# Reordering the first batch of a fused attention and phase-mixing kernel

## The chip, the cores and the metric

The kernel runs on one core of one Trainium2 chip, in one launch. The metric is the device time of that launch in microseconds. Times before are 173.44, 174.29 and 175.55 us; the median is 174.29 us.

## The reference

There are two stages. The first is attention over `q`, `k`, `v` of shape (4 batches, 8 heads, 768 positions, 64 channels), in which a query sees only the first 8 keys (the global ones) and the 96 keys up to its own position. Each head subtracts a slope times the distance from the scores.

```python
scores = scale * (q @ k.T) - slope[h] * dist      # dist = n_local for global keys out of the band
scores = where(is_global | is_local, scores, -1e9)
x = softmax(scores) @ v                           # heads side by side: (4, 768, 512)

theta = x @ w_theta
y = w_tok_r @ (x * cos(theta)) + w_tok_i @ (x * sin(theta))   # over the 768 positions
u = x + y
out = u + maximum(u @ w_ch, 0)
```

## The kernel before, in words

**Tiles.** Positions are dealt to 128 partitions, six to each, so a head pair's q or k is a tile of 128 rows by 2 x 384 columns. TensorE transposes it into `qT` and `kT` (channels of the two heads on the partitions). `GROUPS` splits the band of scores of a head pair into three groups of 128x128 blocks: group 0 (three blocks), groups 1 and 2 (four blocks each). A block is either the diagonal one or the one before it. For the blocks before the diagonal of query tiles 2 to 5, `kT` has four extra tiles of 128 columns (`kT[:, S:]`): a copy of key tiles 1 to 4 with the first 8 columns overwritten by the global keys (`att_extras`, lines 231 to 238, the "key copies"). `prepare_v` (lines 88 to 94) makes the same kind of copy of v, `v_pv`.

**Weights of the scores.** Distances come into the scores in one of two ways. In batch 0, groups 0 and 2 get a bias on TensorE (`att_bias`, line 252, with the scaled identities `ident_d`), then ScalarE makes the exponential `p` (line 275). Everywhere else ScalarE makes the exponential `e` (line 279) and VectorE multiplies it by `wmask` (`att_mul`, lines 290 and 292).

**Stages of a head pair.** `att_transpose` (transposes on line 215, copies out of PSUM on line 225, kT by ScalarE, qT by VectorE), key copies, `att_scores` for three groups, `att_values` (line 319), `att_norm` (lines 335, 337) and `turn_x` (line 351), which turns the result for the product with `w_theta` (`mix_theta`, line 368). ScalarE makes cosine and sine (lines 376, 377), VectorE `mix_z` (line 384). `setup_wtok` turns the two position weights into `w_tokT` (TensorE line 114, copy line 117 by VectorE or line 119 by ScalarE). `mix_tok` (line 403) and `mix_ch` (line 445) are the large products.

**Order.** Each operation goes through `K`, which keeps the written order on its engine: the lists at lines 506 to 576 (batch 0) and 578 to 604 are the schedule. `attend_beside` weaves the next batch's attention into the products of this one. Tiles named with `bufs=2` have two places; a third allocation waits until the first is read for the last time. Those that matter here are `ps_w` (wide score and theta tiles), `ps_tr` (transposes), `ps_mm`, and `kT`.

**Loads.** The first head pair of q and k comes as f32 over the SP and ScalarE queues (line 142) and is cast by VectorE (line 509). All other loads are issued by GpSimd (lines 75, 80, 102) on one queue, in the order of lines 153 to 158, then `load_wtok(0)`, `load_wtok(1)`, batch 1, `w_ch`. GpSimd also makes most key copies, between those issues. `keep_warm` (line 137) issues matmuls on zeros.

Of the kernel before, what the change touches and what calls it, by code (L numbers as in the profile page):

```python
# [16 lines left out]
def kernel(  # L17
# [13 lines left out]
    nc = tc.nc  # L31
# [72 lines left out]
    def load_wtok(wi):  # L104
        w_nats[wi] = mbuf.tile([T, NT, S], BF, name="w_nat", tag="zri", bufs=3)
        load_weight(w_nats[wi], (moe_w_tok_r, moe_w_tok_i)[wi])
# [34 lines left out]
    for src, dst, queue in ((q, first[:, 0], nc.sync), (k, first[:, 1], nc.scalar)):  # L141
        K(queue.dma_start(out=dst, in_=src[0, 0:2].rearrange("h (p t) d -> p h (t d)", t=NT)))
# [7 lines left out]
    keep_warm(8)  # L150
# [80 lines left out]
    def att_extras(b, h0, eng=nc.gpsimd, values=True):  # L231
        kT = kTs[b, h0]
        K(eng.tensor_copy(out=kT[:, S:], in_=kT[:, T:S - T]))  # L233
        K(eng.tensor_copy(
            out=kT[:, S:].rearrange("a (t p) -> a t p", p=T)[:, :, 0:NG],
            in_=kT[:, None, 0:NG].to_broadcast([T, NT - 2, NG])))
        if eng is nc.gpsimd and values:
            prepare_v(b, h0)
# [16 lines left out]
    def att_scores(b, h0, g_, mul=True):  # L255
# [3 lines left out]
        bias = b == 0 and g_ != 1  # L259
# [246 lines left out]
    for h in range(H):  # L506
        make_wmask(h)
# [3 lines left out]
    att_transpose(0, 0, extras=False, between=lambda: keep_warm(1), cuts=(43, T))  # L511
    make_ident_d(2, 6)
    att_extras(0, 0, nc.vector)
    prepare_v(0, 0, nc.vector)
    keep_warm(1)
    att_scores(0, 0, 0)
    att_scores(0, 0, 1)
    att_transpose(0, 2, extras=False)
# [4 lines left out]
    for h0 in (2, 4, 6):  # L523
        att_scores(0, h0, 0)
        att_scores(0, h0, 1, mul=False)
        att_values(0, h0 - 2, apart=True)
        att_norm(0, h0 - 2)
        att_norm(0, h0 - 1)
        if h0 < 6:
            att_transpose(0, h0 + 2)  # L530
            if h0 == 2:
                load_wtok(1)
            else:
                load_heads(1, 0, 4)
        att_mul(0, h0, 1)
        att_scores(0, h0, 2)
        if h0 < 6:
            turn_x(0, h0 // 2 - 1, False)
# [3 lines left out]
    turn_x(0, 2, False, nc.scalar.copy)  # L542
# [26 lines left out]
    setup_wtok(1, 3, "dve", False)  # L569
# [3 lines left out]
    mix_tok(0, 0, [(4, 0), (5, 0), (2, 1), (3, 1)])  # L573
    mix_tok(0, 1, [(4, 0), (5, 0), (2, 1), (3, 1)])
    setup_wtok(1, 4, "dve", False)
    setup_wtok(1, 5, "dve", False)
# [63 lines left out]
```

## Time and profile before

| what | value |
|---|---|
| median of three runs | 174.29 us |
| the profiled execution's own time | 173.54 us |
| its span, first to last instruction | 171.8 us |
| TensorE busy (matmul) | 162.1 us, 94% |
| VectorE / ScalarE / GpSimd busy | 114.2 / 103.0 / 60.9 us |
| granted TensorE clock | 1.000 over the span |

Times are microseconds from the first instruction; "idle before" is time in which an engine had nothing to do, with the instruction that ended it. PE is the matmul side of TensorE, PEld its weight loads, DVE VectorE, ACT ScalarE, POOL GpSimd, SP the engine of the other DMA queue. [...] 1.7 us of the profiled time (173.54 less 171.8) lie around the span.

### The profile page before, as it was taken

The numbers are of one execution on the slowest core, as the hardware profiler recorded it, in microseconds if no ns is written. First come the engines' busy times: TensorE is split into PE (matmuls) and PEld (weight loads), VectorE is DVE, ScalarE is ACT, GpSimd is POOL, SyncE is SP. The second block draws the span as 40 slices with busy tenths as digits, with TensorE's granted clock in tenths as the row PEclk, the third lists the DMA queues.
The fourth block names the chain that finished last, engine by engine and source line by source line (L and its number), as shares of the span: only waits on it lengthen the run. The fifth ranks groups of instructions, "written<-read, shape, count | busy, mean of one in ns | idle before, by whom it ended". The sixth has DMA issues, their size and how long they took to land.

```text
span 171.8 us, 4076 instructions
## 1 busy us (share of the span) xinstructions
PE 162.1 (94%) x1700; PEld 87.5 (51%) x1700; DVE 114.2 (67%) x210; ACT 103.0 (60%) x120; POOL 60.9 (35%) x99
## 2 busy tenths in 40 slices
PE   7669999999999999999999998999999999999992
PEld 2246665556465654536556553545655544444441
DVE  7878865965858774767587694748567766634362
ACT  5969887947676562798658604798756708400010
POOL 8996797004672820033944700044134000000000
PEclk9999999999999999999999999999999999999999
DMA  5999999999999999910699999911433642233325
GB/s 151 188 170 189 209 211 209 196 183 179 173 142 148 114 229 199 250 64 4 81 167 118 152 210 197 213 65 22 89 77 94 84 152 86 96 34 61 103 109 185
DMA packets 57058, 24.05 MB, mean 140 GB/s; under 512 B 43088, under 2 KB 54096, under 8 KB 57040
## 3 DMA queue, kind: packets, MB, share of 16 engines
q0 software_dynamic: 35328, 12.45, 69.2%
q1 hardware_dynamic: 21440, 10.95, 29.6%
q10 hardware_dynamic: 272, 0.39, 0.7%
q8 instruction: 13, 0.21, 0.6%
q14 instruction: 5, 0.04, 0.1%
HBM read 25.69 MB, written 6.29 MB: 186 GB/s over the span
## 4 chain that ended last, share of the span: by engine, by line
PE 76%; DMA 9%; DVE 6%; POOL 3%; ACT 2%; issue 2%; DVEq 0%; POOLq 0%; ACTq 0%
PE ps_mm L403 34%; PE ps_mm L445 11%; PE ps_w L368 10%; PE ps_w L270 6%; PE ps_tr L215 6%; DMA uTd<-u 5%; PE ps_w L319 4%; DMA v_sb<-in_v_dram 4%; DVE w_tokT L117 2%; PE ps_mm L319 2%; PE ps_tr L114 1%; DVE zri L384 1%; ACT e L279 1%; DVE p L292 1%; ACT kT L225 1%
## 5 line engine op out<-in xcount | busy, mean ns | idle before, releaser
L403 PE MATMUL ps_mm<-zri,w_tokT 128*128 128x512 bf16 x288 | 68.7, 380 | 0.1
L279 ACT ACTIVATE e<-ps_w 128x1024 bf16<-128x1024 f32 (+1 forms) x40 | 37.1, 958 | 18.4 <-PE ps_w L270 18.4
L403 PEld LDWEIGHTS <-w_tokT 128*128 128x128 bf16 x288 | 26.2, 98 | 30.7 <-issue 2.3
L233 POOL COPY kT<-kT 128x512 bf16<-128x512 bf16 x15 | 9.6, 643 | 68.8 <-ACT kT L225 68.7
L292 DVE TENSOR_TENSOR p<-e,wmask 128x1024 bf16<-128x1024 bf16 x28 | 19.9, 709 | 12.2 <-ACT e L279 12.2
L376 ACT ACTIVATE cs<-ps_w,halfpi 128x1024 bf16<-128x1024 f32 x12 | 13.4, 1116 | 19.9 <-PE ps_w L368 19.8
L408 DVE TENSOR_TENSOR u<-x_sb,ps_mm 128x512 bf16<-128x512 bf16 x24 | 16.2, 683 | 12.5 <-PE ps_mm L403 12.5
L368 PE MATMUL ps_w<-w_theta_bf,xT 128*128 128x512 bf16 x96 | 22.8, 379 | 0.3 <-ACT cs L377 0.3
L445 PE MATMUL ps_mm<-w_ch_bf,uTd 128*128 128x512 bf16 x88 | 22.5, 379 | 0.5 <-DMA uTd<-u 0.5
L384 DVE TENSOR_TENSOR zri<-cs,x_sb 128x1024 bf16<-128x1024 bf16 x24 | 16.1, 690 | 9.7 <-ACT cs L376 8.4
L270 PE MATMUL ps_w<-qT,kT 64*128 64x128 bf16 (+1 forms) x320 | 16.0, 223 | 2.8 <-DVE qT L225 1.3
L448 DVE SCALAR_TENSOR_TENSOR o_sb<-ps_mm,u 128x512 f32<-128x512 f32 (+2 forms) x25 | 16.5, 665 | 1.1 <-PE ps_mm L445 0.9
L270 PEld LDWEIGHTS <-kT 64*128 64x128 bf16 x320 | 9.3, 94 | 12.8 <-issue 8.5
L225 ACT COPY kT<-ps_tr 128x768 bf16<-128x768 bf16 (+2 forms) x17 | 12.9, 765 | 2.9 <-PE ps_tr L215 2.8
L319 PEld LDWEIGHTS <-p 128*128 128x128 bf16 x352 | 12.7, 97 | 3.7 <-DVE p L292 0.5
L368 PEld LDWEIGHTS <-xT 128*128 128x128 bf16 x96 | 8.9, 98 | 10.9 <-issue 0.5
L445 PEld LDWEIGHTS <-uTd 128*128 128x128 bf16 x88 | 8.1, 97 | 9.9 <-DMA uTd<-u 1.2
L80 POOL DMA_DIRECT2D v_sb<-in_v_dram x10 | 13.1, 1309 | 0.0
L377 ACT ACTIVATE cs<-ps_w 128x1024 bf16<-128x1024 f32 x12 | 12.2, 1020 | 0.0
L327 DVE TENSOR_TENSOR x_sb<-ps_w,rec 128x768 bf16<-128x768 f32 x12 | 11.5, 958 | 0.4
L319 PE MATMUL ps_w<-v_sb,p 128*128 128x65 bf16 x168 | 10.3, 193 | 0.0
L430 ACT COPY uT<-ps_tr 128x512 bf16<-128x512 bf16 x1 | 0.6, 586 | 15.5 <-PE ps_tr L426 15.5
(79 smaller groups left out, 189.5 us busy)
## 6 DMA issues: line engine op xcount, KB each, us to landing
out_dram<-o_sb SPq DMA_DIRECT2D x23, 256.0 KB, 3.0
q_sb<-in_q_dram POOLq DMA_DIRECT2D x6, 384.0 KB, 7.7
k_sb<-in_k_dram POOLq DMA_DIRECT2D x6, 384.0 KB, 10.4
v_sb<-in_v_dram POOLq DMA_DIRECT2D x6, 384.0 KB, 15.1
w_nat<-in_moe_w_tok_r_dram POOLq DMA_DIRECT2D x1, 1152.0 KB, 12.5
w_nat<-in_moe_w_tok_i_dram POOLq DMA_DIRECT2D x1, 1152.0 KB, 13.6
v_sb<-in_v_dram POOLq DMA_DIRECT2D x4, 192.0 KB, 7.2
q_sb<-in_q_dram POOLq DMA_DIRECT2D x3, 192.0 KB, 6.7
```

The costliest lines, as they stand in the source:

```text
L225: K(op(out=dst.rearrange("a (p t) -> a p t", t=NT)[:, p0:p1, :], in_=src.rearrange("a (t p) -> a p t", t=NT)[:, p0:p1, :]))
L270: K(nc.tensor.matmul(ps[:, hh, i_ * T:(i_ + w) * T], lhsT=kT[R, kc:kc + T], rhs=qT[R, it * T:(it + w) * T], start=not bias, stop=not bias ...
L279: K(nc.scalar.activation(e[:, :, 0:n * T], ps[:, :, 0:n * T], AF.Exp, scale=scale))
L292: K(nc.vector.tensor_mul(p.rearrange("a h (r x) -> a h r x", r=2), e.rearrange("a h (r x) -> a h r x", r=2), wmask[:, hs, None, T:3 * T].t ...
L319: K(nc.tensor.matmul(dst, lhsT=lhsT, rhs=rhs, start=(i_ == 0), stop=(i_ == len(mms) - 1)))
L368: K(nc.tensor.matmul(pth[:, s2, :], lhsT=xTs[b][:, dc, c:c + T], rhs=w_theta_bf[:, dc, :], start=(dc == 0), stop=(dc == NC - 1)))
L376: K(nc.scalar.activation(cs[:, :, 0, :], pth, AF.Sin, bias=halfpi))
L384: K(nc.vector.tensor_mul(zris[b][:, st:st + 2, wi, :].rearrange("a s (c d) -> a s c d", d=T), cs[:, :, wi, :].rearrange("a s (c d) -> a s ...
L403: K(nc.tensor.matmul(acc, lhsT=w_tokT[wi][:, st, tt * T:(tt + 1) * T], rhs=zris[b][:, st, wi, :], start=(done[b, tt] == 0), stop=(done[b, ...
L408: K(nc.vector.tensor_add(us[b][:, tt, :].rearrange("a (c d) -> a c d", d=T), x_sb[b][:, :, tt, :], acc.rearrange("a (c d) -> a c d", d=T)))
L445: K(nc.tensor.matmul(pc[:, 0:N], lhsT=uT[:, c:c + T], rhs=w_ch_bf[:, dc, cols], start=(dc == 0), stop=(dc == NC - 1)))
L448: K(nc.vector.scalar_tensor_tensor(o_sb, in0=pc[:, 0:N], scalar=0.0, in1=us[b][:, tt, cols], op0=ALU.max, op1=ALU.add))
```

## The change

All of it but the last hunk is in batch 0's attention.

- The first loads of q and k are split by head: head 0 on the SP queue, head 1 on the ScalarE queue, q ahead of k on both. Seven warm matmuls are issued instead of eight.
- `att_transpose(0, 0)` cuts its copies at column 64 of 128 instead of 43, and its key copies are made in two parts of two tiles each.
- Only six of eight `wmask` are made ahead; the last two stand behind the first scores and behind the transposes of pair 4.
- Pair 0's v copies on VectorE stand behind the transposes of pair 2; the scaled identities are made in two portions at other places.
- While pairs 2 and 4 are at their scores, the transposes of the next pair stand ahead of `att_values` of the pair before, not behind it. In pair 0 the multiplication of group 1 moves behind the transposes of pair 2.
- Pair 6's group 0 has no bias: it is multiplied by `wmask` on VectorE.
- `turn_x(0, 0)` and `(0, 1)` stand later, and `turn_x(0, 2)` is copied by VectorE instead of ScalarE.
- Two of the `w_tokT` copies go from VectorE to ScalarE, and the last two are set up four matmuls earlier.

```diff
+    for src, dst in ((q, first[:, 0]), (k, first[:, 1])):
+        for hh, queue in enumerate((nc.sync, nc.scalar)):
+            K(queue.dma_start(out=dst[:, hh, :], in_=src[0, hh].rearrange("(p t) d -> p (t d)", t=NT)))
...
-    keep_warm(8)
+    keep_warm(7)
...
+    def att_extras(b, h0, eng=nc.gpsimd, values=True, parts=1):
+        n = (NT - 2) // parts
+        for t0 in range(0, NT - 2, n):
+            dst = kT[:, S + t0 * T:S + (t0 + n) * T]
+            K(eng.tensor_copy(out=dst, in_=kT[:, (t0 + 1) * T:(t0 + 1 + n) * T]))
+            K(eng.tensor_copy(out=dst.rearrange("a (t p) -> a t p", p=T)[:, :, 0:NG],
+                in_=kT[:, None, 0:NG].to_broadcast([T, n, NG])))
...
-        bias = b == 0 and g_ != 1
+        bias = b == 0 and (g_ == 2 or g_ == 0 and h0 < H - 2)
...
-    for h in range(H):
+    for h in range(6):
         make_wmask(h)
...
-    att_transpose(0, 0, extras=False, between=lambda: keep_warm(1), cuts=(43, T))
-    make_ident_d(2, 6)
-    att_extras(0, 0, nc.vector)
-    prepare_v(0, 0, nc.vector)
-    keep_warm(1)
-    att_scores(0, 0, 0)
-    att_scores(0, 0, 1)
-    att_transpose(0, 2, extras=False)
+    att_transpose(0, 0, extras=False, between=lambda: keep_warm(1), cuts=(64, T))
+    keep_warm(1)
+    att_extras(0, 0, nc.vector, parts=2)
+    make_ident_d(2, 2)
+    att_scores(0, 0, 0)
+    make_wmask(6)
+    att_scores(0, 0, 1, mul=False)
+    att_transpose(0, 2, extras=False)
+    att_mul(0, 0, 1)
+    prepare_v(0, 0, nc.vector)
+    make_ident_d(4, 4)
     att_extras(0, 2, nc.gpsimd, False)
     prepare_v(0, 2)
     load_wtok(0)
     att_scores(0, 0, 2)
+    for h0 in (2, 4):
         att_scores(0, h0, 0)
         att_scores(0, h0, 1, mul=False)
+        att_transpose(0, h0 + 2)
+        if h0 == 2:
+            make_wmask(7)
+            load_wtok(1)
+        else:
+            load_heads(1, 0, 4)
         att_values(0, h0 - 2, apart=True)
+        att_mul(0, h0, 1)
         att_norm(0, h0 - 2)
         att_norm(0, h0 - 1)
         att_scores(0, h0, 2)
+        if h0 == 4:
+            turn_x(0, 0, False)
+    att_scores(0, 6, 0)
+    att_scores(0, 6, 1, mul=False)
+    turn_x(0, 1, False)
+    att_values(0, 4, apart=True)
+    att_norm(0, 4)
+    att_norm(0, 5)
+    att_mul(0, 6, 1)
+    att_scores(0, 6, 2)
...
-    turn_x(0, 2, False, nc.scalar.copy)
+    turn_x(0, 2, False)
...
-    setup_wtok(1, 3, "dve", False)
+    setup_wtok(1, 3, "act", False)
...
     mix_tok(0, 0, [(4, 0), (5, 0), (2, 1), (3, 1)])
+    setup_wtok(1, 4, "dve", False)
+    setup_wtok(1, 5, "act", False)
     mix_tok(0, 1, [(4, 0), (5, 0), (2, 1), (3, 1)])
-    setup_wtok(1, 4, "dve", False)
-    setup_wtok(1, 5, "dve", False)
```

More of the change, by code (lines that the diff above doesn't have):

```diff
@@ L140 @@
     first = mbuf.tile([T, 2, 2, NT * D], FP, name="first", tag="zri", bufs=3)
-    for src, dst, queue in ((q, first[:, 0], nc.sync), (k, first[:, 1], nc.scalar)):
-        K(queue.dma_start(out=dst, in_=src[0, 0:2].rearrange("h (p t) d -> p h (t d)", t=NT)))
+    for src, dst in ((q, first[:, 0]), (k, first[:, 1])):
+        for hh, queue in enumerate((nc.sync, nc.scalar)):
+            K(queue.dma_start(out=dst[:, hh, :],
+                              in_=src[0, hh].rearrange("(p t) d -> p (t d)", t=NT)))
     K(nc.scalar.activation(halfpi_e, halfpi, AF.Exp))
@@ L229, in att_transpose @@
             att_extras(b, h0)
-    def att_extras(b, h0, eng=nc.gpsimd, values=True):
+    def att_extras(b, h0, eng=nc.gpsimd, values=True, parts=1):
         kT = kTs[b, h0]
[L233 to L236, printed above, removed]
+        n = (NT - 2) // parts
+        for t0 in range(0, NT - 2, n):
+            dst = kT[:, S + t0 * T:S + (t0 + n) * T]
+            K(eng.tensor_copy(out=dst, in_=kT[:, (t0 + 1) * T:(t0 + 1 + n) * T]))
+            K(eng.tensor_copy(
+                out=dst.rearrange("a (t p) -> a t p", p=T)[:, :, 0:NG],
+                in_=kT[:, None, 0:NG].to_broadcast([T, n, NG])))
         if eng is nc.gpsimd and values:
@@ L522 @@
     att_scores(0, 0, 2)
-    for h0 in (2, 4, 6):
+    for h0 in (2, 4):
         att_scores(0, h0, 0)
         att_scores(0, h0, 1, mul=False)
+        att_transpose(0, h0 + 2)
[4 more added lines that the diff above has]
+            load_heads(1, 0, 4)
         att_values(0, h0 - 2, apart=True)
+        att_mul(0, h0, 1)
         att_norm(0, h0 - 2)
         att_norm(0, h0 - 1)
[L529 to L535, printed above, removed]
-        att_scores(0, h0, 2)
-        if h0 < 6:
-            turn_x(0, h0 // 2 - 1, False)
+        att_scores(0, h0, 2)
+        if h0 == 4:
[8 more added lines that the diff above has]
+    att_scores(0, 6, 2)
     load_heads(1, 4, 4)
```

## The prediction

> **What bounds the kernel now.** I read the windows first. From 40 to 168 us TensorE is busy 127.02 of 128 us (127.42 of the sum row less 0.40 of the last window) at full clock, with the same large products behind the change as before it. So what the change is worth is the shift of TensorE's work at about 45 us, and nothing that happens ahead of it counts unless it is still there then.
>
> ```profile
> sum 132.00, PE 127.42 PEld 66.92 DVE 84.71 ACT 72.08 POOL 34.06; mean PE 3.86 PEld 2.03 DVE 2.57 ACT 2.18 POOL 1.03
> 168.00:172.00 4.00, 0.40 (x5) 0.21 (x3) 0.76 (x2) 0.00 (x0) 0.00 (x0) 0.97 0.48 174
> ```
>
> Then the chain that ended last, at its start. The reader is to see that v of pair 0 lands at 9.53 and that VectorE's queue, in order, puts the v copies and a multiplication ahead of pair 2's qT, for which TensorE waits until 12.52 us.
>
> ```profile
> 3.03 6.50 DMA v_sb<-in_v_dram
> ...
> 9.55 0.72 DVE v_pv L91
> ...
> 10.29 0.71 DVE v_pv L92
> 11.01 0.59 DVE p L292
> 11.60 0.88 DVE qT L225
> ...
> 12.52 0.56 PE ps_w L270 x12
> ```
>
> Third the timeline of GpSimd (start, length). Its DMA issues follow one another from 1.48 to 10.89 us; only then comes pair 2's key copy, though kT has been ready since 10.92 at the latest.
>
> ```profile
> 9.05 1.08 POOL L80 DMA_DIRECT2D v_sb<-in_v_dram  x1
> 10.07 0.82 POOL L102 DMA_DIRECT2D w_theta_bf<-in_moe_w_theta_dram  x1
> 10.99 1.08 POOL L233 COPY kT<-kT 128x512 bf16<-128x512 bf16 x1
> 12.13 0.21 POOL L234 COPY kT<-kT 128x32 bf16<-128x32 bf16 x1
> ```
>
> Last ScalarE's timeline at the seam to batch 1: it is idle 2.3 us, copies kT, loads the table for Exp, and the first exponential waits for TensorE, not for the table.
>
> ```profile
> 37.78 0.80 ACT L225 COPY kT<-ps_tr 128x768 bf16<-128x768 bf16 x1 [2.30 <-PE ps_tr L215]
> 38.60 1.28 ACT L279 ACT_TABLE_LOAD   x1
> 40.50 0.81 ACT L279 ACTIVATE e<-ps_w 128x768 bf16<-128x768 f32 x1 [0.62 <-PE ps_w L270]
> 41.73 1.94 ACT L279 ACTIVATE e<-ps_w 128x1024 bf16<-128x1024 f32 x2 [0.42 <-PE ps_w L270]
> ```
>
> **The start, to 12.3 us.** The four first loads carry the same bytes; q's halves now lead on both queues. q landed 4.3 us after its issue at 0.74, k 4.6; with q first it lands between 3.9 (half of the bytes) and 5.05 (no gain), and k stays at 5.34. VectorE is busy with the identities until 4.28 anyway. The second issue on ScalarE's queue costs 0.48 us, ahead of a first `wmask` that waits for `dist` until 3.61 while the table load and dummy end at 2.74: hidden with 0.4 us to spare. k's cast ends at 5.95 instead of 6.33, k's transposes at about 6.55. ScalarE, which before made eight masks until 7.02, makes six (0.426 us each) until 6.2 and is free then. kT's parts of 384 columns: between the 0.38 us of 258 columns and the roughly 0.5 of 510, so 7.05 and 7.46. Key copies in parts let group 1 begin at 7.6 instead of 8.77. But mask 6 (0.43) now stands ahead of its exponential: that starts at 8.6 instead of 9.21, and kT of pair 2 is ready at 10.3 instead of 10.92. VectorE no longer waits for v here: qT of pair 2 is ready at 9.35 instead of 12.47, and group 0 of pair 2 runs at 10.4 instead of 12.52.
>
> There the next wait takes over. Group 1 of pair 2 needs GpSimd's key copies, which cannot begin before 10.89: by the rows they end at 12.34, or 11.85 if the large copy takes 0.61 as later copies do (VectorE's two-input multiplication is no longer beside it). Before, this group ran at about 12.8. So up to 3.1 us gained on VectorE become 0.4 to 0.9 on TensorE, and it hardly matters how early q lands.
>
> **12.3 to 27.5 us.** I follow the order with the rows' paces: exponential 0.92 (four blocks) or 0.71 (three), kT 0.74, qT 0.86, multiplication 0.65, the four norm operations 1.42, turned copy 0.48 on VectorE; TensorE 0.79 for 24 transposes, 0.76 for a bias and eight scores, 0.75 for values, 0.34 for a turn.
> Group 1 of pair 2 ends 12.75; pair 4's q and k have landed (11.93 and 12.92), transposes to 13.55, exponential 12.8 to 13.8, kT 14.5 (before 15.54). Mask 7 (0.43) fits into ScalarE's wait for group 2, whose scores end at 15.05 behind the values. Group 0 of pair 4 15.4 to 15.75; group 1 waits for a `ps_w` place (group 2's exponential, 16.12), runs at 16.17 against 16.88. Transposes of pair 6 16.5 to 17.3 (k landed 16.14), kT 18.45 (before 19.77). Group 0 of pair 6 at 19.15, without its two bias matmuls (0.32 us saved), group 1 at 19.9 (before 21.11), exponentials of pair 6 to 21.5 (before 22.74).
> Now VectorE binds: behind the exponential of group 0 at 20.57 it has the added multiplication (0.55), a turned copy (0.48), norms 1.42, multiplication 0.65, then the turned copy taken over from ScalarE (0.5): 24.2. Norms of pair 6 begin at 24.15 instead of 24.73, the last turn at 25.75 instead of 26.3, theta ends 27.5 instead of 28.2. Of 1.2 us at 21 us, **0.6 us** is left: two VectorE operations, 1.05 us, stand on the path there; their cover, VectorE's two waits of 0.53 before values, is used up.
>
> **27.5 to 40 us** has the same chain of sines, `zri` and weight copies, so the shift stays. The landings leave room: `w_tok_r` 26.03 for 27.4, `w_tok_i` 31.6 for 32.8, batch 1's k 35.5 for 36.6. The copy of weight tile 3 on ScalarE falls into its 2.3 us of idleness and costs nothing.
>
> **The seam.** Weight tiles 4 and 5, set up four matmuls earlier, take away TensorE's two short waits there (0.04 and 0.08 us idle in the windows of half a microsecond from 40 to 41). But tile 5's copy by ScalarE (0.75) now stands between kT and the table load. With the shift of 0.6 it runs 38.7 to 39.45, the load to 40.74, first exponential to 41.56. Group 2 needs that tile's `ps_w` place, so it starts at 41.6, no earlier than before; the two next exponentials end at 43.4 against 43.68, the multiplication behind them at 44.1, and values at 44.15 instead of 44.45. **0.6 becomes 0.27**; with the faster GpSimd copy 0.8 becomes 0.47. I take 0.3.
>
> The loads at 1.25 and 25.21 us last 1.28 and the next activation follows 0.01 us behind, so I add no pause behind the load. [...]
>
> **Sum.** The profiled execution took 173.54 us: 171.8 of span and 1.7 around it. Less 0.3 that is 173.2. Its time lies 0.75 under the median; against 174.29 I forecast **174.0 us**.
>
> **Rivals.**
> 1. *The earlier gain survives the seam.* If ScalarE's copy of tile 5 runs without delaying the table (kT copied earlier), the shift at values is the full 0.6 to 0.8 and the two waits at 40 us (0.1) go: 0.7 to 0.9 us, or, if VectorE's added 1.05 is hidden too, up to 1.4; no more, since batch 1's k at 35.5 stops it. 172.9 to 173.6, taken as 173.4. For it: the idle 2.3 us on ScalarE. Against: the load stands last in the order. Chance 0.2.
> 2. *Slower: VectorE between 20.6 and 24.2 us.* The same instructions took 0.93 and 0.96 us (multiplications at 15.83 and 20.02) while GpSimd copied, against 0.67. If the three operations there run at such a pace, 0.3 each, the shift at 28 us falls from 0.6 to -0.3, and the seam's 0.33 comes on top: 0.6 us slower, 174.9. It decides from the point where less than 0.33 of shift is left at 37 us. For it: GpSimd's v copies for pair 6 run until 21. Against: they end before most of that strip. Chance 0.25.
> 3. *The change moves nothing*: GpSimd's issues last longer, group 1 of pair 2 stays at 12.8, and the seam is no later because the copy fits: 174.3. Chance 0.1.
> 4. *A pause behind the Exp load.* That load ended at 39.88 and its exponential began at 40.50, so a pause of up to 0.62 isn't excluded there; it would now be on the path: 0.3 gained less 0.62 is 0.3 us slower, 174.6. The two other loads speak against it; chance 0.02.
>
> The forecast itself has 0.43. 1% here, 1.7 us, is about what a measurement of this kernel can tell from no change: the three runs lie 2.1 us apart. All cases are inside it; what lies beyond is the scatter of the median and an unknown cost at either side. Faster by over 1%: 0.06; within: 0.85; slower: 0.09. The range holds rivals 1 to 3 and half a microsecond of scatter on either side: 172.7 to 175.2.
>
> **What would show it.** Pair 2's first scores near 10.4, its group 1 at 11.9 to 12.4 behind GpSimd's small copy; TensorE idle 1.2 to 1.7 us between them; theta's last product of the first four columns near 27.5; the Exp table load near 39.5 with an exponential right behind it; values of batch 1 near 44.1. I am wrong if the table load isn't what the first exponential waits for, if the first 45 us are shifted by over a microsecond, or if TensorE has new waits behind them.

## The result, and the profile after

The changed kernel takes 174.14 us (median of 22 runs, 173.68 to 175.46), the kernel before, run beside it, 173.33 us (22 runs, 172.83 to 175.55). The ratio is 1.0043, with an interval of 1.0024 to 1.0061: the change makes the kernel **0.75 us slower** (0.42 to 1.06), where 0.3 us faster was forecast. That the forecast of 174.0 us lies near 174.14 is luck: the median of the three runs of before that it was set against lay 1 us above the median of 22. The profiled execution of after took 174.62 us, with a span of 172.7.

The windows of after, in the same form as those shown of before (window, its length, then busy time and instructions of PE, PEld, DVE, ACT, POOL, granted clock, DMA share, GB/s):

```profile
40.00:168.00 128.00, 124.06 (x1216) 65.97 (x1235) 82.43 (x133) 72.74 (x81) 33.51 (x57) 1.00 0.88 122
168.00:172.00 4.00, 0.93 (x8) 0.47 (x6) 1.25 (x3) 0.00 (x0) 0.00 (x0) 1.00 0.54 200
```

TensorE is 3 us less busy than before in the same 128 us, but the trace also holds 30 matmul records fewer (1216 for 1246), so this difference can't be read as waiting. What is new is read from the waits of TensorE instead, here from 20 to 70 us of after (engine, tile and line, what was waited for: us in total, times, longest):

```profile
PE ps_w L275 <- ACT e L284: 1.0, 1, 1.0
PE ps_mm L450 <- DMA uTd<-u: 1.0, 1, 1.0
PE ps_w L275 <- ACT p L280: 0.5, 1, 0.5
```

The first is the seam, where the forecast had put a wait until 41.6 us. The second is new at this place: before has its wait for a `uTd` tile, 0.5 us, at 104.84 us.

The chain that ended last, up to 14 us, and its piece at 59 us (start, us, what):

```profile
7.58 0.81 ACT p L280
8.39 0.41 ACT wmask L195
8.80 0.91 ACT e L284
9.72 0.69 ACT kT L227
10.41 1.64 ACT p L280 x2
12.04 0.04 issue
12.08 0.40 PE ps_w L275 x8
...
59.21 9.06 DMA uTd<-u
```

v and VectorE's v copies have left the chain, as the change means them to. Pair 2's group 1 (12.08) now ends a row of ScalarE's work. GpSimd's timeline shows that its key copies were ready at nearly the same moment (12.02):

```profile
9.12 1.06 POOL L80 DMA_DIRECT2D v_sb<-in_v_dram  x1
10.14 0.79 POOL L102 DMA_DIRECT2D w_theta_bf<-in_moe_w_theta_dram  x1
10.89 0.66 POOL L238 COPY kT<-kT 128x512 bf16<-128x512 bf16 x1
11.61 0.41 POOL L239 COPY kT<-kT 128x32 bf16<-128x32 bf16 x1
```

At the seam, ScalarE's timeline has tile 5's copy ahead of the table load, and the three exponentials stand right behind it, without the waits for TensorE that before had there:

```profile
37.09 0.80 ACT L227 COPY kT<-ps_tr 128x768 bf16<-128x768 bf16 x1 [0.92 <-PE ps_tr L217]
38.67 0.80 ACT L119 COPY w_tokT<-ps_tr 128x768 bf16<-128x768 bf16 x1 [0.78 <-PE ps_tr L114]
39.49 1.28 ACT L284 ACT_TABLE_LOAD   x1
40.78 2.64 ACT L284 ACTIVATE e<-ps_w 128x768 bf16<-128x768 f32 x3
```

So in this one execution the hand sum is met almost to the tenth up to 45 us: pair 2's group 0 at 10.47 (10.4 forecast), its group 1 at 12.08 (11.85 to 12.34), theta's last product of the first four columns at 27.35 (27.5), the table load at 39.49 (39.5). Scores of batch 1's pair 2 begin at 44.87 us, in before at 45.11: a gain of 0.24, where 0.27 was forecast. Yet the kernel is slower. That the sum is met is partly two small misses that cancel: batch 1 begins 0.69 us earlier where 0.6 was forecast, and the seam takes 0.45 of it where 0.33 was forecast. The experiments ask where the gain went, and whether it was there.

**How the traces are compared.** Three stretches separate the places of the change, each read from the starts of instruction groups on TensorE. The *start* is when batch 1's pair 0 is transposed (36.82 in before, 36.13 in after). The *seam* is from there to the transposes of its pair 4 (10.95 and 11.40 us). The *tail* is from the start of the last four transposes of u to the end of the span (171.8 less 165.99, 5.81 us, and 172.7 less 166.51, 6.19 us). What lies between seam and tail has the same products in the same order. By these stretches the spans differ by 0.69 gained at the start, 0.45 lost at the seam, 0.78 between seam and tail (all of it in waits for `uTd`, 1.46 us in after and 0.68 in before) and 0.38 in the tail.

### The profile page after: what moved, and what is told of

The parts are those of the page before. It is cut to its first block, busy times and chain, and to the rows that moved or that the text cites. A ratio compares the mean times of both kernels' runs of the same rounds, so it can differ in the third digit from the quotient of the medians.

```text
span 172.7 us, 4057 instructions
## 1 busy us (share of the span) xinstructions
PE 160.1 (93%) x1674; PEld 86.9 (50%) x1697; DVE 114.0 (66%) x212; ACT 103.1 (60%) x121; POOL 60.2 (35%) x99
## 2 busy tenths in 40 slices
DMA packets 57090, 24.05 MB, mean 139 GB/s; under 512 B 43120, under 2 KB 54128, under 8 KB 57072
## 3 DMA queue, kind: packets, MB, share of 16 engines
q0 software_dynamic: 35328, 12.45, 67.6%
q1 hardware_dynamic: 21456, 10.95, 29.8%
## 4 chain that ended last, share of the span: by engine, by line
PE 75%; DMA 10%; ACT 5%; DVE 5%; issue 3%; DVEq 0%; ACTq 0%
PE ps_mm L408 32%; DMA uTd<-u 10%; PE ps_w L373 9%; PE ps_mm L450 9%; PE ps_tr L217 7%; PE ps_w L275 6%; PE ps_w L324 4%; ACT p L280 3%; PE ps_mm L137 2%; PE ps_mm L324 2%; PE ps_tr L114 2%; DVE zri L389 1%; DVE w_tokT L117 1%; PE ps_w L257 1%; ACT e L284 1%
## 5 line engine op out<-in xcount | busy, mean ns | idle before, releaser
L408 PE MATMUL ps_mm<-zri,w_tokT 128*128 128x512 bf16 x276 | 67.2, 380 | 1.1 <-issue 0.6
L284 ACT ACTIVATE e<-ps_w 128x1024 bf16<-128x1024 f32 (+1 forms) x41 | 37.7, 955 | 17.3 <-PE ps_w L275 17.3
L297 DVE TENSOR_TENSOR p<-e,wmask 128x1024 bf16<-128x1024 bf16 x28 | 19.3, 691 | 11.8 <-ACT e L284 11.7
L450 PE MATMUL ps_mm<-w_ch_bf,uTd 128*128 128x512 bf16 x81 | 21.5, 379 | 1.8 <-DMA uTd<-u 1.0
L324 PEld LDWEIGHTS <-p 128*128 128x128 bf16 x352 | 12.8, 97 | 3.4 <-DVE p L297 0.3
L227 ACT COPY kT<-ps_tr 128x768 bf16<-128x768 bf16 (+1 forms) x17 | 12.9, 767 | 1.4 <-PE ps_tr L217 1.4
L295 DVE TENSOR_TENSOR p<-e,wmask 128x768 bf16<-128x768 bf16 x13 | 7.3, 565 | 7.2 <-ACT e L284 7.2
L324 PE MATMUL ps_w<-v_sb,p 128*128 128x65 bf16 x168 | 10.2, 193 | 0.0
## 6 DMA issues: line engine op xcount, KB each, us to landing
k_sb<-in_k_dram POOLq DMA_DIRECT2D x6, 384.0 KB, 10.2
```

Of the source, the lines that this page charges most:

```text
L284: K(nc.scalar.activation(e[:, :, 0:n * T], ps[:, :, 0:n * T], AF.Exp, scale=scale))
L297: K(nc.vector.tensor_mul(p.rearrange("a h (r x) -> a h r x", r=2), e.rearrange("a h (r x) -> a h r x", r=2), wmask[:, hs, None, T:3 * T].t ...
L324: K(nc.tensor.matmul(dst, lhsT=lhsT, rhs=rhs, start=(i_ == 0), stop=(i_ == len(mms) - 1)))
L408: K(nc.tensor.matmul(acc, lhsT=w_tokT[wi][:, st, tt * T:(tt + 1) * T], rhs=zris[b][:, st, wi, :], start=(done[b, tt] == 0), stop=(done[b, ...
L450: K(nc.tensor.matmul(pc[:, 0:N], lhsT=uT[:, c:c + T], rhs=w_ch_bf[:, dc, cols], start=(dc == 0), stop=(dc == NC - 1)))
```

## Experiments

In all of them the kernel before ran on the same chip, and each ratio is to it. "After's code" in a front or a seam means that the part in question is as in the change.

### e1, e2: is the loss the wait for u's fourth tile?

`uTd` of tile 4 is turned by a DMA that landed 9.06 us after its issue in after. e1 and e2 give it more time: the channel product of tile 4 moves one step back, in before (e1) and in after (e2).

```diff
-        mix_ch(b, 4)
         mix_theta(b + 1, 2)
+        mix_ch(b, 4)
         mix_z(b + 1, 2)
```

> The kernel before, with the channel product of token tile 4 of a batch put behind the theta products of the next two tiles instead of between them. Theory 'u4': the turned copy of u tile 4, a DMA issued 8 to 9 us earlier, lands at the moment its product starts (67.25 for 67.41 us in batch 0, 104.80 for 104.33 in batch 1). With 1.73 us more room the waits of 0.5 us go and the time falls by 0.3 to 0.6 us below the kernel before. Rival 'spread': the waits for this DMA are not what separates kernels; the time stays within 0.2 us of before.

> The changed kernel with the same move of the channel product of tile 4. Theory 'u4': the change gained 0.24 us up to 66 us and lost 1.16 us at one place, the wait for u tile 4's turned copy (0.99 us of matmul idleness at 68.32). With more room that loss goes: this kernel is 1.0 to 1.4 us faster than the changed one in its trace, 0.5 to 0.8 us faster than the kernel before, and 0.15 to 0.3 us faster than the kernel before with the same move. Rival 'spread': the loss is made up of many small waits or of a later one; this kernel stays 0.5 us or more slower than the kernel before with the same move.

e1: 172.58 us (ratio 0.9971, 0.9953 to 0.9988). e2: 173.35 us (1.0020, 0.9997 to 1.0044). Neither trace has a wait for `uTd` left. The wait costs both kernels about the same, 0.70 us of the medians in before (173.28 to 172.58) and 0.79 in after (174.14 to 173.35). Without it after's code is still 0.77 us behind before's. **The wait for `uTd`, the most visible new row of the profile, isn't what the change costs**: 0.75 us with the waits, 0.77 without them.

With the waits gone the two traces can be set beside each other (us):

| stretch | e1 (before's code) | e2 (after's code) | difference |
|---|---|---|---|
| start: batch 1 pair 0 transposed | 36.49 | 36.51 | 0.02 |
| seam, to pair 4 | 10.95 | 11.39 | 0.44 |
| from pair 4 to the last four transposes of u | 117.53 | 117.53 | 0.00 |
| tail, to the span's end | 5.83 | 6.17 | 0.34 |
| span | 170.8 | 171.6 | 0.8 |

The 0.8 us stand in two places, the seam and the tail, and the start isn't earlier. The other runs test these three lines.

### e3, e4: the seam alone, and the change without it

e3 is before with the last hunk of the change, e4 the change without it.

```diff
-    setup_wtok(1, 3, "dve", False)
+    setup_wtok(1, 3, "act", False)
 ...
+    setup_wtok(1, 4, "dve", False)
+    setup_wtok(1, 5, "act", False)
     mix_tok(0, 1, [(4, 0), (5, 0), (2, 1), (3, 1)])
-    setup_wtok(1, 4, "dve", False)
-    setup_wtok(1, 5, "dve", False)
```

> The kernel before with the last hunk alone: w_tokT tile 3 of the second weight copied by ScalarE, tiles 4 and 5 set up four matmuls earlier, 5 copied by ScalarE. By the prediction's sum for the seam the Exp table load moves from 38.6 to about 40.1 and batch 1's first values from 44.45 to 44.8: 0.33 us later at that point. Theory 'u4' says that the end also depends on where the DMA for u tile 4 then lands, so the time may differ from +0.33 by up to a microsecond either way; its trace shows the seam by itself. Rival: the seam costs nothing, because the first exponential waits for TensorE and not for the table; values stay at 44.45.

> The changed kernel without its last hunk. By the prediction's sum the shift of 0.6 us (0.7 in its trace) at 37 us is kept through the seam: values of batch 1 near 43.7, 0.5 us ahead of the changed kernel. Theory 'u4': the end depends on the wait for u tile 4; if that wait is as long as in the changed kernel the time is 173.6, if it grows by what was gained it is 174.1, if it goes it is 172.5. Rival 'spread': 0.5 us faster than the changed kernel whatever the wait.

e3: 174.00 us (1.0048, 1.0029 to 1.0067), that is 0.72 us slower than before. e4: 173.59 us (1.0031, 1.0008 to 1.0054), 0.55 faster than after. The seam stretch is 11.39 us in e3 and 10.95 in e4. ScalarE at e3's seam:

```profile
38.94 0.80 ACT L119 COPY w_tokT<-ps_tr 128x768 bf16<-128x768 bf16 x1 [0.78 <-PE ps_tr L114]
39.76 1.28 ACT L279 ACT_TABLE_LOAD   x1
41.05 2.64 ACT L279 ACTIVATE e<-ps_w 128x768 bf16<-128x768 f32 x3
```

The copy waits 0.78 us for tile 5's transposes and delays the load: the first exponential starts at 41.05, where before, moved to e3's start, would have 40.09 (40.50 less the 0.41 by which batch 1 starts earlier). The seam costs 0.44 us of TensorE time whether batch 0 is changed or not.

### e5: the change with the first loads of before

```diff
-    for src, dst in ((q, first[:, 0]), (k, first[:, 1])):
-        for hh, queue in enumerate((nc.sync, nc.scalar)):
-            K(queue.dma_start(out=dst[:, hh, :], in_=src[0, hh]...))
+    for src, dst, queue in ((q, first[:, 0], nc.sync), (k, first[:, 1], nc.scalar)):
+        K(queue.dma_start(out=dst, in_=src[0, 0:2]...))
```

> The changed kernel with the first loads of q and k as before: one transfer each, q on one queue, k on the other. By the prediction it hardly matters how early q lands, since GpSimd's issues until 10.9 us gate the next step: batch 0 to theta within 0.1 us of the changed kernel, time 174.0 to 174.2. Rival: the extra transfers disturb the later queues (in the two traces with split first loads and no room, u tile 4's turned copy took 8.9 and 9.1 us, in the others 7.6 to 8.3); then it is 0.5 to 1 us faster than the changed kernel and u tile 4 lands under 8.3 us after its issue.

173.91 us (1.0045, 1.0017 to 1.0073). The times spread: seven runs lie between 173.23 and 173.97, five between 174.4 and 175.4, so the median says little. The trace (of 173.23) says two things. The q of the first pair is transposed at 5.69 us instead of 5.04, and yet batch 1 starts at 36.09 (36.13 in after): the earlier q bought nothing in these two executions, since both wait for GpSimd's key copies before pair 2's group 1 (12.04 and 12.08). And the tail is 5.82 (before 5.81, after 6.19). The two transfers at 1 us lengthen the last 6 us of the kernel.

### e6: does the place of u's turn in time decide?

After with two matmuls on zeros (0.40 us in its trace) ahead of the seam's end, which shift everything behind it.

```diff
+            if b == 1 and h0 == 0:
+                keep_warm_tr(2)
```

> The changed kernel with two matmuls on zeros added behind the first values of batch 1, 0.43 us of work for nothing on TensorE. Theory 'phase': a kernel that issues the turn of u tile 3 by 53.55 us meets the value load of batch 2 (landing 63.0), one that issues it at 53.75 or later does not (landing 60.6 to 61.2), and only the first kind has u tile 4 late. With the delay that turn is issued at about 53.95, the load lands by 61.3, the wait of 1 us at u tile 4 falls under 0.4, and the kernel is not slower than the changed one, 173.5 to 174.1. Rival: the wait belongs to the early issues of the weight loads or to the split first loads; then it stays at 0.7 to 1.0 us and the kernel takes 174.3 to 174.6.

174.62 us (1.0076, 1.0047 to 1.0104), by the medians 0.48 slower than after, about the time that was added. In the profiled run, the fastest of the six, the waits for `uTd` are shorter (0.23 and 0.52 us, by the stretches they lengthen, for 1.16 and 0.30 in after), and its span is 0.3 us shorter than after's. But all six runs (174.33 to 175.31) lie above after's median, where the theory "phase" had put them at or below it. So the idea that after's loss is an unlucky phase of the turn isn't borne out.

### e7, e8: the later channel product with either repair of the seam

e7 is e2 with the old seam, e8 is e2 with tile 5 set up early but copied by VectorE. This is e8's edit at the seam:

```diff
     setup_wtok(1, 4, "dve", False)
-    setup_wtok(1, 5, "act", False)
+    setup_wtok(1, 5, "dve", False)
     mix_tok(0, 1, [(4, 0), (5, 0), (2, 1), (3, 1)])
```

> The changed kernel without its last hunk and with the late channel product of tile 4. Theory 'seam and u4': the two losses of the change are the table load at the seam (0.45 us) and the wait for u tile 4, so without both this runs 0.4 to 0.55 us faster than the changed kernel with the late product (173.35), that is 172.8 to 172.95, and within 0.35 us of the kernel before with the late product (172.58). If the front of the change gained the 0.6 us that its first trace shows, it is 172.2 or less instead.

> The changed kernel with the late channel product of tile 4 and with one word changed at the seam: w_tokT tile 5 is copied by VectorE, not ScalarE, in its new early place. Theory 'seam': the loss there is that ScalarE's copy stands ahead of the Exp table load; with it on VectorE the load starts right behind kT and batch 1's values come 0.4 to 0.6 us earlier than in the changed kernel; 172.7 to 172.95. Rival: the loss is the early place on TensorE, which makes the tiles' transposes wait; then it stays at 173.35.

e7: 172.72 us (0.9977, 0.9952 to 1.0002). e8: 172.40 us (0.9952, 0.9931 to 0.9974). The seam takes 10.95 us in e7 and 10.58 in e8. ScalarE at e8's seam:

```profile
37.70 0.80 ACT L227 COPY kT<-ps_tr 128x768 bf16<-128x768 bf16 x1 [0.92 <-PE ps_tr L217]
38.51 1.28 ACT L284 ACT_TABLE_LOAD   x1
40.41 2.81 ACT L284 ACTIVATE e<-ps_w 128x768 bf16<-128x768 f32 x3 [0.62 <-PE ps_w L275]
```

The load starts right behind kT again, the scores are what the exponential waits for, and the earlier set-up now gains 0.37 us. So one operation makes the difference between 0.44 lost and 0.37 gained: which engine copies tile 5.

### e9, e10: the repairs together, with either batch 0

e9 is e8 with the first loads of before. e10 is before with the same repairs (tile 3 by ScalarE, tiles 4 and 5 set up early, both by VectorE; channel product of tile 4 late) and its own batch 0.

> The changed kernel with tile 5's copy on VectorE, the late channel product of tile 4, and the first loads as before (one transfer each). All six traces with split first loads end 6.17 to 6.24 us after the start of the last turn of u (the four transposes of line 426 or its counterpart), all four with unsplit ones 5.76 to 5.83 us. Theory 'tail': the two extra transfers cost 0.37 us there and nothing else; this runs at 172.0 (172.40 less 0.37), 1.2 to 1.4 us faster than before. Rival: the tail is a matter of chance or of the order of batch 0; then it stays at 172.4.

> The kernel before with the last hunk (tile 5's copy on VectorE instead of ScalarE) and the late channel product of tile 4; batch 0's attention and the first loads as before. By the seam's sum it gains 0.37 us on the kernel before with the late product alone (172.58): 172.2. Against the same with the changed batch 0 (the run with the first loads as before) it measures what all of batch 0's reordering is worth by itself: by the traces 0.2 us (start of batch 1's transposes 36.34 on the mean of seven against 36.57 on the mean of three), by the prediction 0.6, by rival 'nothing' 0.

e9: 173.55 us (0.9969, 0.9939 to 0.9999), in two groups: four runs from 171.76 to 172.09 and eight from 173.54 to 173.61. e10: 172.20 us (0.9922, 0.9893 to 0.9950), five runs from 171.86 to 172.50 and one at 175.0, which is the profiled one. The profiled run of e9 is one of the late group. TensorE in it, from 4 us on (start, length, what):

```profile
4.30 0.82 PE L255 MATMUL ps_w<-dist,ident_d 128*128 128x384 bf16 x2
5.69 0.85 PE L215 MATMUL ps_tr<-ident,q_sb 128*64 128x128 bf16 x12 [0.57 <-DVE q_sb L512]
...
11.13 1.03 PE L255 MATMUL ps_w<-dist,ident_d 128*128 128x512 bf16 x2
...
14.51 0.50 PE L215 MATMUL ps_tr<-ident,k_sb 128*64 128x128 bf16 x12
```

Twelve transposes take 0.85 us at 5.7 us and 0.50 at 14.5, and two bias matmuls at 11.13 still take 1.03 (0.60 in e17): TensorE runs at a lower pace until about 13.7 us, in e10's profile until about 13.9, and batch 1 starts at 37.91 and 39.31 us instead of 36.1 to 36.9. In before the bias at 4.55 us took 0.49 and the first q transposes 0.53. That raised a new suspect, the seven warm matmuls instead of eight (e13 to e18).

### e11, e12: is it the number of early transfers, or whose turn it is?

In the traces of before and after the transfers of the SP and ScalarE queues (56 and 58) take eight completion semaphores in turn, and from the second round on a wait for its own semaphore stands ahead of each issue (all 48 in before, all 50 in after). The end of SP's instruction list in the built programs of before and after, with the semaphore (the eight are DMAHW0 to DMAHW7):

```
before  L450 DMACopy out_dram<-o_sb 128x384 [waits DMAHW6_49,DVE_49]
        L450 DMACopy out_dram<-o_sb 128x128 [waits DMAHW7_49,DVE_49]
after   L455 DMACopy out_dram<-o_sb 128x384 [waits DMAHW0_49,DVE_49]
        L455 DMACopy out_dram<-o_sb 128x128 [waits DMAHW1_49,DVE_49]
```

Two more transfers at the start move the last output from the eighth semaphore to the second. e11 is before with one more first transfer (q's split by head, both on SP), e12 with eight more (q and k in five pieces by partition), after which the turn is where it was.

```diff
e11
-        K(queue.dma_start(out=dst, in_=src[0, 0:2]...))
+        for h0_, n_ in (((0, 1), (1, 1)) if src is q else ((0, 2),)):
+            K(queue.dma_start(out=dst[:, h0_:h0_ + n_, :], in_=src[0, h0_:h0_ + n_]...))
e12
-        K(queue.dma_start(out=dst, in_=src[0, 0:2]...))
+        from_ = src[0, 0:2]...
+        for p0, p1 in ((0, 32), (32, 64), (64, 96), (96, 112), (112, 128)):
+            K(queue.dma_start(out=dst[p0:p1], in_=from_[p0:p1]))
```

> The kernel before with only q's first load split by head, both parts on the SP queue: one transfer more on the queues of SP and ScalarE. The program gives those transfers eight completion semaphores in turn; the last output has the eighth in the kernel before, the first here, the second in the changed kernel. Theory 'turn': the program's end waits for the eight in order, so each that stands behind the last output's costs some 0.06 us: the tail from the last turn of u is 5.8 + 7 x 0.06 = 6.2 to 6.3 us. Rival 'number': each extra transfer costs 0.19 us; the tail is 6.0.

> The kernel before with q's and k's first loads in five pieces each by partitions (32, 32, 32, 16, 16): eight transfers more on the queues of SP and ScalarE, so that the last output has the eighth semaphore again. Theory 'turn': the tail is 5.8 us as before. Rival 'number': 8 x 0.19 us more, 7.3. What the pieces do to the start of batch 0 is not at issue here.

The tail is 6.28 us in e11 and 5.77 in e12: one more transfer lengthens it, eight more don't. The eight kernels that have the change's first loads show 6.13 to 6.24 (mean 6.19); ten others with the first loads of before 5.75 to 5.84 (mean 5.79). In the tail everything up to the last output's issue is the same. Timeline of before's end, from the last transposes (start, length, what):

```profile
165.97 3.57 SPq L450 DMA_DIRECT2D out_dram<-o_sb  x5
165.99 0.39 PE L426 MATMUL ps_tr<-ident,u 128*128 128x128 bf16 x4
```

and of after's:

```profile
166.50 3.57 SPq L455 DMA_DIRECT2D out_dram<-o_sb  x5
166.51 0.39 PE L431 MATMUL ps_tr<-ident,u 128*128 128x128 bf16 x4
```

The last issue ends 3.55 and 3.56 us after the transposes' start, the span 2.26 us later in before (169.54 to 171.8) and 2.63 in after (170.07 to 172.7). So the turn costs about 0.37 us behind the last issue. The views leave out instructions that wait for semaphores, but the kept traces hold them, and there SP waits for the eight one after another, in the order of the turn, before the program ends (us):

| trace | semaphore of the last output | wait for it passed | waits behind it | all passed |
|---|---|---|---|---|
| before | eighth | 170.89 | none | 170.95 |
| e12 | eighth | 176.71 | none | 176.77 |
| after | second | 171.44 | six | 171.87 |
| e11 | first | 170.64 | seven | 171.13 |

From the end of the last issue to the moment when its own semaphore is passed all four take the same, 1.33 to 1.37 us. The waits that come ahead of it pass while the transfer is under way; those behind it cost 0.06 us each, though their transfers have landed by then (in after by 170.58 us). From the last output's semaphore to the end of the waits it is 0.065 us in all ten traces with the first loads of before and 0.43 us in all eight with those of the change. So the 0.37 us are these six waits.

The times of e11 and e12 hold more than the tail: 175.11 us (1.0094, 1.0060 to 1.0128) and 179.59 us (two runs; 1.0352, 1.0307 to 1.0396). In e12 q came late, and its trace shows what that does:

```profile
4.58 0.85 PE L254 MATMUL ps_w<-dist,ident_d 128*128 128x384 bf16 x2
9.54 0.85 PE L217 MATMUL ps_tr<-ident,q_sb 128*64 128x128 bf16 x12 [4.12 <-DVE q_sb L511]
```

TensorE waited 4.12 us for q, and the granted clock was 0.50 from 8.9 to 19.2 us (0.967 over the span). e11's profiled run is its fastest (173.75); why seven of its eight runs lie above 174 isn't known.

### e13, e14, e15: warm matmuls

e13 is e9 with eight warm matmuls instead of seven, e14 the change with eight, e15 is e10 with ten instead of eight. The edit of e13 and e14:

```diff
-    keep_warm(7)
+    keep_warm(8)
```

> e9's kernel with eight warm matmuls instead of seven, nothing else. Theory "warm" (the seventh-to-eighth matmul decides when TensorE comes to full pace): the first bias pair takes 0.49 us instead of 0.82 as in the traces of the kernels with eight, and the group of times at 173.55 disappears, so that the median is 171.8 to 172.2, a ratio of about 0.992. Rival "phase" (the time at which TensorE comes to full pace depends on something that runs free of the kernel): two groups again, at 171.9 and 173.55, though perhaps in other shares; median anywhere between.

> The changed kernel with eight warm matmuls instead of seven, nothing else. Theory "no part of it" (the slow start lies behind the wait for GpSimd's key copies at 12 us in nearly all executions): the time stays at 174.1, a ratio to the kernel before of 1.003 to 1.006, since seam and tail (0.44 and 0.37) are untouched. Rival "warm": the batch-1 transposes come 0.2 us or more earlier than in the change's traces (36.1 to 36.7) and the time falls by as much or more, to 173.3 to 173.8, a ratio at or below 1.002.

> e10's kernel (the kernel before, with weight tiles 4 and 5 set up earlier and copied by VectorE, and the channel product of tile 4 a step later) with ten warm matmuls instead of eight. They add 0.4 to 0.8 us of TensorE time ahead of the first bias, behind which the first transposes wait for kT's inputs until about 5 us, so they should be hidden. Theory "warm": no run near 173.5 or 175, all within 171.8 to 172.5, median 172.0, ratio about 0.992. Rival "phase": one run in some six is again 1.7 us or more later, median as e10's 172.2.

e13: 172.17 us (0.9938, 0.9925 to 0.9951), all six runs from 171.94 to 172.32. e14: 174.71 us (1.0094, 1.0061 to 1.0127), from 173.97 to 176.87. e15: 172.05 us (0.9929, 0.9916 to 0.9941), all five from 171.84 to 172.09. The time of the change doesn't fall with the eighth matmul, so the missing one isn't what it lost. e13 has no late group any more, but its first bias still takes 0.85 us, which the theory "warm" had excluded: the eighth matmul didn't bring TensorE to full pace by then (it came at 6.75 us).

The profiled run of e14 (176.87) shows a second stretch at the lower pace, and this one the granted clock does name (it is the column before the last two):

```profile
12.00:14.00 2.00, 1.07 (x24) 0.74 (x26) 1.58 (x6) 1.65 (x2) 1.92 (x4) 0.89 1.66 189
14.00:16.00 2.00, 2.00 (x35) 1.81 (x34) 1.52 (x4) 1.21 (x2) 0.78 (x2) 0.50 1.91 180
16.00:18.00 2.00, 1.97 (x17) 0.60 (x15) 0.91 (x3) 0.70 (x2) 1.88 (x5) 0.76 1.45 200
```

By the trace's clock records it lasts from 13.6 to 17.0 us. TensorE had waited 1.09 us for GpSimd's key copies, until 12.48, and waited 0.44 us for k as the clock fell, until 13.85. Pair 6 is transposed at 18.72 us (16.26 in after) and batch 1 starts at 38.59.

### e16, e17, e18: what batch 0's new order is worth

All with ten warm matmuls: e16 is e9's kernel, so that beside e15 only the order of batch 0 differs; e17 is before, e18 the change.

> e9's kernel (the change's batch 0, with the first loads of before, tile 5 of the position weights copied by VectorE, the channel product of tile 4 a step later) with ten warm matmuls. Beside e15 (172.05) only the order of batch 0 differs. Theory "gain" (the rearranged batch 0 brings what the hand sum gave, 0.3 to 0.7 us at 37 us): 171.4 to 171.8, all runs within 0.4 us. Rival "nothing" (the gate at GpSimd's key copies and VectorE behind it take it all): 171.9 to 172.2.

> The kernel before with ten warm matmuls instead of eight. Theory "clean start": as fast as the kernel before or 0.1 to 0.4 us faster (172.9 to 173.3), batch 1's transposes at 36.2 to 36.5, and a narrower spread. Rival: the two more matmuls stand in the way of the first bias and it is 0.2 to 0.4 us slower.

> The changed kernel with ten warm matmuls instead of seven. Theory "seam and tail" (0.44 and 0.37, less 0.1 of the front): 173.6 to 174.0, that is 0.6 to 0.9 us above e17; the tail from the last four transposes is 6.2 us. Rival "cold start" (the change's loss comes from the longer stretch at half pace that seven warm matmuls leave): within 0.3 us of e17.

e16: 172.12 us (0.9924, 0.9901 to 0.9948), beside 0.9929 (0.9916 to 0.9941) of e15: **"nothing" fits: the 0.6 us that the new order of batch 0 was to bring doesn't show.** The two intervals together leave room for a gain of up to half a microsecond; the traces below show none (36.46 and 36.41 us on the mean). e17: 173.33 us (0.9999, 0.9975 to 1.0024). e18: 174.57 us (1.0069, 1.0040 to 1.0098), 1.24 above e17; "cold start" would have put it within 0.3, and "seam and tail" was too low by 0.3. The profiled run of e18 is its slowest (175.85). Its span is 2.4 us longer than e17's (173.9 and 171.5), and the stretches give it: start 0.69 (36.87 less 36.18), seam 0.44 (11.39 less 10.95), the two waits for `uTd` 0.9 (1.6 and 0.7 us in the waits), tail 0.38 (6.16 less 5.78).

The start of 0.69 shows how the front works. All traces that weren't at the lower pace beyond 7.1 us are here, with the moment at which TensorE passes pair 2 (in before's code the start of groups 0 and 1, which run together; in after's code that of group 1):

| batch 0 as in before | pair 2 | batch 1 | batch 0 as in after | pair 2 | batch 1 |
|---|---|---|---|---|---|
| before | 12.52 | 36.82 | after | 12.08 | 36.13 |
| e1 | 12.20 | 36.49 | e2 | 12.27 | 36.51 |
| e3 | 12.11 | 36.41 | e4 | 12.42 | 36.51 |
| e11 | 12.10 | 36.40 | e5 | 12.04 | 36.09 |
| e15 | 11.88 | 36.17 | e6 | 12.09 | 36.14 |
| e17 | 11.88 | 36.18 | e7 | 12.19 | 36.24 |
| | | | e8 | 12.45 | 36.74 |
| | | | e13 | 12.50 | 36.55 |
| | | | e16 | 12.78 | 36.84 |
| | | | e18 | 12.82 | 36.87 |
| **mean** | 12.12 | 36.41 | | 12.36 | 36.46 |

From pair 2 on both orders run like clockwork: 24.3 us to batch 1 in all six traces of before's code, 24.05 to 24.09 us in eight of the ten of after's (24.24 in e2, 24.29 in e8). What varies lies ahead of 12.8 us, and **before's profile was the latest of its six**. (The two groups differ in one thing more: TensorE came to full pace by 5.4 us in all six of before's code, but later in all of after's except e2 and e5. Those two start batch 1 at 36.51 and 36.09, so this hardly hides a gain of 0.6.) VectorE in it:

```profile
9.55 0.71 DVE L91 COPY v_pv<-v_sb 128x520 bf16<-128x520 bf16 x1 [0.83 <-DMA v_sb<-in_v_dram]
10.29 0.71 DVE L92 COPY v_pv<-v_sb 8x520 bf16<-8x520 bf16 x1
10.93 0.67 DVE L292 TENSOR_TENSOR p<-e,wmask 128x1024 bf16<-128x1024 bf16 x1
11.53 0.94 DVE L225 COPY qT<-ps_tr 128x768 bf16<-128x768 bf16 x1
```

and in e15:

```profile
8.92 0.30 DVE L91 COPY v_pv<-v_sb 128x520 bf16<-128x520 bf16 x1 [0.21 <-DMA v_sb<-in_v_dram]
9.26 0.29 DVE L92 COPY v_pv<-v_sb 8x520 bf16<-8x520 bf16 x1
10.26 0.69 DVE L292 TENSOR_TENSOR p<-e,wmask 128x1024 bf16<-128x1024 bf16 x1 [0.72 <-ACT e L279]
10.87 0.95 DVE L225 COPY qT<-ps_tr 128x768 bf16<-128x768 bf16 x1
```

The same v lands 0.63 us earlier and its two copies take 0.30 and 0.29 us instead of 0.71 each. Then VectorE waits for ScalarE's exponential, not for v, and qT is ready 0.65 us earlier. The wait for v, on which the change was built, is in this execution not there. And what follows is the same in both codes: GpSimd's key copies, which the rest of pair 2 needs. In the six traces of before's code they end 11.86 to 12.34 us, within 0.13 us of qT, so without any wait for qT no more would be gained than the about 0.3 us of group 0's scores, which could then run ahead of them. In after's ten they end 11.98 to 12.76, latest where ScalarE's kT is late; in e18:

```profile
11.65 0.65 POOL L238 COPY kT<-kT 128x512 bf16<-128x512 bf16 x1 [0.68 <-ACT kT L227]
12.36 0.40 POOL L239 COPY kT<-kT 128x32 bf16<-128x32 bf16 x1
```

## Why the prediction was wrong

**The sum, term by term** (us, minus is faster):

| term | forecast | shown by the runs |
|---|---|---|
| start, at 37 us | -0.6 | 0.05 (means of 16 traces); none by time, within half a microsecond (e15, e16) |
| seam | 0.33 | 0.44 (six traces with it, seven without); 0.55 and 0.72 by the times of e4 and e3 |
| more first transfers | 0 | 0.39 (18 traces with e11 and e12 beside them) |
| sum | -0.27 | 0.88; measured 0.75 (0.42 to 1.06) |

**The step that failed first is "Before, this group ran at about 12.8", and with it "12.3 to 27.5 us", where "0.6 us is left".** As arithmetic it was right: after's trace shows 0.69. But it is a difference to one execution of before, and took that one's v copies (0.71 each) and v's landing (9.53) for properties of the kernel. The wait "until 12.52 us" ends at 11.88 to 12.20 in five other traces. That GpSimd's key copies take over as the next wait was right; but in before's code they end at nearly the same moment as the wait that the change removes, so on the mean batch 1 begins 0.05 us later with the new order, not 0.6 earlier. The page's own rows held a hint: the key copy beside them took 1.08 us where later ones took 0.61. I used that for the after side of the sum (11.85 instead of 12.34) and didn't ask what a before with 0.61, and quicker v copies, would look like. Rival 3 said the front moves nothing because group 1 of pair 2 stays where it is, and that half of it came true.

**"The start, to 12.3 us" costed the extra first transfers at nothing** but the time of their issue on the queues. At 1 us no cost shows (batch 1 starts at 36.13 us in after and at 36.09 in e5, which lacks them). They shift the turn of eight completion semaphores for the 54 later transfers, and 0.39 us appear at 170 us, 0.37 of them as six waits of SP behind the last output's. No step of the prediction looked at the other end of the kernel, and I wrote that only what still stands at 45 us counts. That sentence is the failed reasoning: it holds for TensorE's work and not for what the change does to a shared order of resources.

**The seam was right in its mechanism and a quarter too small.** The first exponential was put at 40.74 (forecast) and came at 40.78; group 2 at 41.6 and came at 41.64. The stretch to pair 4 is 0.44 longer instead of 0.33. The forecast of 44.15 for the values was met (44.07).

**Rivals.** Rival 1 (the table not delayed) would have needed VectorE for tile 5's copy; e8 is that kernel, and gains 0.37 there. Rival 2 (VectorE from 20.6 to 24.2 us) isn't seen: the multiplication at 22.84 us takes 0.68 us in after, not 0.93 or 0.96, and from pair 6's transposes to batch 1 after's code takes 19.87 or 19.88 us in six traces (after, e8, e9, e13, e14, e16). Rival 4 (a pause behind the Exp load) isn't seen: the load of 39.49 and 1.28 us is followed by the exponential at 40.78. In e3 too, where the exponential's input is ready, it starts 0.01 us behind the load (39.76 and 1.28, then 41.05).

**The wait for `uTd`** that I named as a thing that would make me wrong ("new waits behind them") did appear, and the runs clear it: before pays for it too (e1), and taken away from both it leaves 0.77 us. By the medians it costs 0.70 us in before's code (e1) and 0.79 and 0.87 in after's (e2; e4 to e7). In single traces it stretches the run by 0.5 to 1.1 us in before's code and by 0.7 to 2.0 in after's, which is why one pair of profiles makes it look like the culprit; that after's code pays 0.1 us more, or by these few traces somewhat more than that, isn't excluded.

**Warm matmuls, eight to seven,** I had also costed at nothing. e14 and e18 show no gain from putting them back; whether the late runs of e5 and e9 come from them isn't settled: e13 has no late group, but its first bias is as slow as e9's.

**A kernel that beats both.** Take from the change only ScalarE's copy of tile 3 and the earlier set-up of tiles 4 and 5, copied by VectorE, move the channel product of tile 4 one step back, and leave batch 0 and the first loads as they were: e10 (0.9922, 0.9893 to 0.9950), and with ten warm matmuls e15, 172.05 us (0.9929, 0.9916 to 0.9941), all its runs within 0.25 us.

## What to carry to other kernels

A stall read from one profile may belong to that execution: before a change is built on it, read the same stretch in a second and a third execution, and see which of its rows (here v's landing, 0.63 us earlier in e15, and its copies, 0.30 us instead of 0.71) differ. A DMA that is free where it stands can still cost at the end of the program, by the semaphore that the last transfer gets (here up to seven waits of 0.06 us); the tail behind the last issue is read on every trace. And a new wait in the profile is not the loss until taking it away from both kernels closes the gap.

## What the runs showed of the hardware that wasn't expected

**The turn of completion semaphores sets the length of the end**: 2.26 us behind the last issue with the eighth (before), 2.63 with the second (after), since each semaphore that SP still has to pass behind the last output's costs 0.06 us (above).

**TensorE's pace at the start differs from run to run, and the granted clock of the views doesn't say so.** The first bias pair takes 0.49 or 0.50 us in before, e1, e3, e11, e15 and e17, and 0.82 to 0.85 in after, e4, e6 to e10, e12 to e14, e16 and e18, with seven, eight or ten warm matmuls ahead of it; e2 and e5 lie between (0.57, 0.52). The views give a granted clock of 1.00 for this time in every trace, but the kept traces hold no clock record at all for it, and the views count what has no record as 1.00 (so does the 1.000 over the span in the table of before). The first record, of 1.00, begins where the instructions come to full pace: at 3.99 to 5.32 us in the eight traces with a first bias of 0.49 to 0.57 us, at 5.53 to 7.02 us in ten of those with 0.82 to 0.85 (in e12, one of the ten, no matmul ran at that moment), and at 13.70 us in e9 and 13.93 in e10. In e17 and e16, both with ten:

```profile
1.19 4.35 PE L137 MATMUL ps_mm<-zero 128*128 128x512 bf16 x10 [1.19 <-DVE zero L123]
5.38 0.49 PE L252 MATMUL ps_w<-dist,ident_d 128*128 128x384 bf16 x2
```

```profile
1.19 4.45 PE L137 MATMUL ps_mm<-zero 128*128 128x512 bf16 x10 [1.19 <-DVE zero L123]
5.43 0.85 PE L255 MATMUL ps_w<-dist,ident_d 128*128 128x384 bf16 x2
```

The warm matmuls of 512 columns follow one another at 0.43 us in before and after (ten take 4.45 us in e16 and e18), the products of 512 columns behind them at 0.22. Full pace as late as 13.7 or 13.9 us goes with 1.6 us more in e9 and 3 in e10, 1 to 2% of this kernel. Why kernels with after's batch 0 so often come to full pace later (5.5 us and more), although TensorE's instructions up to there are the same but for the number of warm matmuls, isn't settled: no run shows what decides the moment.

**A wait early on can be followed by a lower clock**: in e12 4.1 us for q, and a granted clock of 0.50 for 10.2 us from 8.9 us on, before that wait ended; in e14 two waits of 1.1 and 0.4 us, and a granted clock of 0.50 for 3.4 us from 13.6 us on. A wait alone doesn't decide it: e8 waited 1.48 us for the key copies at the same place, and its clock stayed at 1.00. That the waits are the cause is argued from the order in time; no run shows it by itself.

**The 9 us of a turned copy**: `uTd` of tile 4 landed 9.06 us after its issue in after's trace, where the last one, issued at 158 us, landed in 2.4.
